# A linear-attention block on one core: the key weights in four transfers instead of three, a shorter dummy matmul, and another order of the first fifteen matmuls and transposes

## The chip, the cores and the metric

The kernel runs on one core of one Trainium2 chip. The time is the device time of one execution in microseconds (us); the profile comes from one profiled execution and gives its span, from the first to the last instruction of the kernel. Engines are named as in the profile: PE is TensorE's matmul, PEld its weight load, DVE is VectorE, ACT is ScalarE, POOL is GpSimd and SP is SyncE. A "q" behind an engine's name (SPq, ACTq) marks the issuing of a transfer by that engine.

## The reference

The block computes linear attention with 32 heads of 20 columns for one sequence of 2048 rows and 640 columns, in bfloat16.

```
qkv = x @ wqkv                      # 2048x640 @ 640x1920, split into q, k, v of 32 heads x 20
phi = lambda t: where(t > 0, t + 1, exp(t)) + 1e-6
pq, pk = phi(q), phi(k)
kv = einsum("bhsd,bhse->bhde", pk, v)
z  = einsum("bhsd->bhd", pk)
o  = einsum("bhqd,bhde->bhqe", pq, kv) / (einsum("bhqd,bhd->bhq", pq, z) + 1e-6)
out = o @ wo
```

## The kernel before, in words

The 2048 rows of x are worked on in 16 row tiles of 128 rows, the 640 inner columns in 5 blocks of 128. A matmul needs x with its columns on the partitions; that form is the tile xT. Row tiles 0 and 1 are loaded as they are (tile xn, L230) and transposed on PE (`transpose_x`, L193 to L213): a low part of two transposes (columns 0 to 255), copied out of PSUM by VectorE (L212), and a high part of three (columns 256 to 639), copied by ScalarE (L209). Rows 256 onwards come as transposing loads on SP's queue (L189).

`k_half` (L284) multiplies a row tile's xT with the key weights Wk: half h (320 of 640 columns) of row tile st, over the inner blocks named in cs. `k_phi` (L298) then applies phi on ScalarE and VectorE. After the keys of all row tiles the kernel accumulates pk and x into a state (L313), computes the queries (L350), forms the product of state, value weights and output weights, divides by the denominator, and multiplies into the output (L572).

Every engine runs its own instructions in the order in which they are written. The class `Plan` notes which instruction wrote and read what, and adds the waits on semaphores. A wait stands ahead of one instruction, and whatever is behind it on that engine waits as well.

What the first microseconds hold:

- `load_wk` (L235) loads x tile 0 ("x01") and x tile 1 ("x12") on SP's queue, and Wk on ScalarE's queue: blocks 0 and 1 in one transfer ("w02"), then blocks 2 and 3 ("w24"), then block 4 ("w45"). Each transfer has its own semaphore. A block of Wk is 128 rows of 640 columns, 160 KB.
- PE first runs dummy matmuls on constants (`warm`, L277): five of 512 columns and one of 256, then the transposes of x tile 0 as they land, then one more dummy of 512 columns (L625).
- Then a written order follows (L626): k and two digits is row tile and inner block, in both halves; a letter a or b behind it picks half 0 or half 1. t1a and t1b are the low and high transposes of x tile 1. Before, it is `k00 k01a t1a k01b t1b k10 k11 k02 k12 k03 k13 k04 k14`. (k01 is row tile 0, inner block 1.)
- K matmuls on inner blocks 0 and 1 of a row tile read the low part of its xT, those on blocks 2 to 4 the high part.

The prediction calls a transpose of the low part "low", one of the high part "high", and the blocks of Wk "block 0" to "block 4".

Of the kernel before, what the change touches and what calls it, by code (L numbers as in the profile page):

```python
# [84 lines left out]
def bass_standalone__linear_attn_block__prompt_kernel(nc, x, wqkv, wo, out):  # L85
# [15 lines left out]
    with contextlib.ExitStack() as ctx:  # L101
# [40 lines left out]
        def bank(b, n=BK, off=0, parts=128):  # L142
            return ps[0:parts, BK * b + off:BK * b + off + n]
# [49 lines left out]
        def transpose_x(st, part):  # L193
            lo, hi = ((0, 2), (2, NC_))[part]
            b = (6, 4)[st] + part
            v = bank(b, HALF).bitcast(BF16)

            def mm(e):
                for c in range(lo, hi):
                    r = e.transpose(  # L200
                        v[:, 128 * c:128 * c + 128],
                        xn[:, st * D + 128 * c:st * D + 128 * c + 128], ident[:, :])
                return r
            P.add("pe", mm, reads=xn_keys(st) + ["ident"], writes=[("bank", b)])
            dst = xT[:, :].rearrange("p (c s) -> p c s", s=S)[
                :, lo:hi, 128 * st:128 * st + 128]
            src = v.rearrange("p (c s) -> p c s", s=128)[:, lo:hi, :]
            if part:
                P.add("act", lambda e: e.copy(dst, src),  # L209
                      reads=[("bank", b), "table"], writes=[("xT", st, lo)])  # L210
            else:
                P.add("dve", lambda e: e.tensor_copy(dst, src),  # L212
                      reads=[("bank", b)], writes=[("xT", st, lo)])  # L213
# [15 lines left out]
        def load_xn(a, b, eng):  # L229
            P.add(eng, lambda e: e.dma_start(  # L230
                xn[:, a * D:b * D].rearrange("p (t n) -> p t n", n=D),
                x[0, 128 * a:128 * b, :].rearrange("(t p) n -> p t n", p=128)),
                writes=[("xn", t) for t in range(a, b)], dma=True)

        def load_wk():  # L235
            tl = mybir.InstLoadActFuncSet(
                name=nc.get_next_instruction_name(),
                act_func_set_id=ACT_TABLE_SET_LN_EXP, ins=[], outs=[])
            P.add("act", lambda e: e.add_instruction(tl), writes=["table"])
            for eng, what in (("sp", "x01 x12"), ("act", "w02 w24 w45")):  # L240
                for k in what.split():
                    a, b = int(k[1]), int(k[2])
                    if k[0] == "x":
                        load_xn(a, b, eng)
                    else:
                        P.add(eng, lambda e, a=a, b=b: e.dma_start(
                            wk[:, a * D:b * D].rearrange("p (c n) -> p c n", n=D),
                            wqkv[128 * a:128 * b, D:2 * D].rearrange("(c p) n -> p c n", p=128)),
                            writes=[("wk", c) for c in range(a, b)], dma=True)
# [27 lines left out]
        def warm(n, cols=BK):  # L277
            for _ in range(n):
                P.add("pe", lambda e: e.matmul(  # L279
                    bank(4, cols), nc.const_aps.tensor(1.0, [128, 128], BF16),  # L280
                    nc.const_aps.tensor(1.0, [128, cols], BF16), start=True, stop=True),
                    writes=[("bank", 4)])
# [333 lines left out]

        pool_const()
        load_wk()
        load_xT()
        load_rest()  # L620
        warm(5)
        warm(1, 256)
        for part in range(2):
            transpose_x(0, part)
        warm(1)  # L625
        order = "k00 k01a t1a k01b t1b k10 k11 k02 k12 k03 k13 k04 k14"  # L626
        for k in order.split():
            st, part = int(k[1]), "ab".find(k[-1])
            if k[0] == "t":
# [127 lines left out]
```

## Time and profile before

| what | value |
|---|---|
| time, median of 3 runs | 99.7 us (99.65 to 99.93) |
| the profiled execution's own time | 99.49 us |
| its span | 98.2 us |
| granted TensorE clock, mean | 1.00 |
| bytes moved | 12.60 MB, 128 GB/s |
| K matmuls (L289) | 160, 22.4 us busy |
| query matmuls (L350) | 95 recorded, 22.0 us busy |
| output matmuls (L572) | 170, 22.1 us busy |
| state matmuls (L313) | 160, 23.2 us busy |

The span leaves out what lies around the kernel's instructions, 1.3 us of the profiled execution's time. A row of the timeline reads: start in us from the span's beginning, duration, engine, line of the kernel, operation, the tile written and the tiles read, shape, and how many instructions are merged in it; where the engine was idle before, the time and what ended it stand in brackets. Matmuls are pipelined: each one's recorded duration is longer than its share of PE's time, so neighbouring rows overlap. In the chain of work that ended last, each piece has its start, its duration and what it is; the chain is followed back from the last instruction, at each step to what released it.

The transfers of the first microseconds, issued and landed by the trace (us):

| transfer | queue | issued | KB | issue to landing |
|---|---|---|---|---|
| x tile 0 | SP | 0.78 | 160 | 2.6 |
| Wk blocks 0, 1 | ACT | 0.80 | 320 | 3.5 |
| x tile 1 | SP | 1.23 | 160 | 3.5 |
| Wk blocks 2, 3 | ACT | 1.29 | 320 | 4.3 |
| Wk block 4 | ACT | 1.82 | 160 | 4.6 |

### The profile page before, as it was taken

What the parts mean: (1) busy time and instruction counts of PE and PEld (TensorE: products, weight loads), DVE (VectorE), ACT (ScalarE), POOL (GpSimd) and SP (SyncE); (2) the same over time, 40 slices, a digit from 0 to 9 for tenths busy, and PEclk for the clock granted to TensorE, in tenths of its full rate; (3) what the DMA queues carried; (4) which work ended last, traced back from release to release, by engine and by line L of the source; (5) the groups of instructions that cost most, each with busy time, mean ns of one, the idle gap of its engine ahead of it and who ended that gap; (6) DMA issues with size and microseconds to landing.
All of it is one profiled execution on the core that took longest, in us unless ns stands there. A gap on an engine that the chain in (4) does not pass through costs nothing.

```text
span 98.2 us, 1813 instructions
## 1 busy us (share of the span) xinstructions
PE 94.8 (97%) x694; PEld 61.1 (62%) x699; DVE 63.7 (65%) x124; ACT 48.8 (50%) x93; POOL 4.7 (5%) x19
## 2 busy tenths in 40 slices
PE   6999999999999999999999999999999999999991
PEld 2467777777755444445687867655557677777771
DVE  5315998898899439997739836759999206272222
ACT  5117455544427120005806456796988665453532
POOL 6400000000000000000000520000000000000000
DMA  2999999999996292000350023313200335532334
GB/s 55 343 263 173 234 211 122 350 366 361 288 166 81 29 256 52 0 0 0 65 75 7 0 63 94 94 33 88 76 0 0 133 81 155 206 124 86 129 133 137
DMA packets 26224, 12.60 MB, mean 128 GB/s; under 512 B 18536, under 2 KB 26216, under 8 KB 26216
## 3 DMA queue, kind: packets, MB, share of 16 engines
q1 hardware_dynamic: 25384, 11.63, 49.9%
q10 hardware_dynamic: 832, 0.86, 2.6%
q8 instruction: 5, 0.08, 0.3%
q14 instruction: 3, 0.02, 0.1%
HBM read 5.90 MB, written 2.62 MB: 87 GB/s over the span
## 4 chain that ended last, share of the span: by engine, by line
PE 92%; DMA 3%; ACT 2%; issue 1%; DVE 0%
PE ps L289 22%; PE ps L572 22%; PE ps L350 22%; PE ps L313 21%; DMA xn<-in_x_dram 3%; ACT w2g L479 2%; PE ps L441 1%; PE ps L540 1%; PE ps L468 1%; PE ps L200 1%; PE ps L279 0%; DVE xT L212 0%; ACT osb L595 0%
## 5 line engine op out<-in xcount | busy, mean ns | idle before, releaser
L313 PE MATMUL ps<-pk,xn 128*128 128x480 bf16 (+1 forms) x160 | 23.2, 299 | 0.0
L289 PE MATMUL ps<-wk,xT 128*128 128x320 bf16 x160 | 22.4, 300 | 0.1
L350 PE MATMUL ps<-xT,wqn 128*128 128x512 bf16 x95 | 22.0, 379 | 0.4 <-issue 0.2
L572 PE MATMUL ps<-w2p,pq 128*128 128x320 bf16 (+2 forms) x170 | 22.1, 291 | 0.0
L572 PEld LDWEIGHTS ps<-w2p,pq 128*128 128x128 bf16 x170 | 15.9, 98 | 6.2 <-issue 0.2
L289 PEld LDWEIGHTS ps<-wk,xT 128*128 128x128 bf16 x160 | 15.7, 98 | 6.5 <-DMA wk<-in_wqkv_dram 0.3
L313 PEld LDWEIGHTS ps<-pk,xn 128*128 128x128 bf16 x160 | 13.6, 98 | 9.4 <-issue 0.3
L358 ACT ACTIVATE eq<-ps 128x512 bf16<-128x512 f32 x20 | 11.9, 597 | 13.8 <-PE ps L350 13.6
L350 PEld LDWEIGHTS ps<-xT,wqn 128*128 128x128 bf16 x100 | 11.4, 118 | 9.1 <-issue 0.3
L302 ACT ACTIVATE ek<-ps 128x640 bf16<-128x640 f32 x16 | 11.2, 704 | 10.5 <-PE ps L289 9.9
L595 ACT CAST osb<-ps 128x320 bf16<-128x320 f32 (+2 forms) x27 | 11.0, 413 | 9.7 <-PE ps L572 8.8
L307 DVE SCALAR_TENSOR_TENSOR pk<-ps,ek 128x640 bf16<-128x640 f32 x16 | 13.2, 825 | 0.5
L565 DVE TENSOR_TENSOR pq<-pq,rd 128x512 bf16<-128x512 bf16 x20 | 7.3, 419 | 4.3 <-DMA rd<-rdc 4.3
L371 DVE TENSOR_SCALAR eq<-eq 128x512 bf16<-128x512 bf16 x20 | 5.7, 287 | 5.9 <-ACT eq L358 5.8
L598 DVE CAST osb<-ps 128x320 bf16<-128x320 f32 (+1 forms) x7 | 3.2, 456 | 8.7 <-PE ps L572 8.7
L304 DVE TENSOR_SCALAR ek<-ek 128x640 bf16<-128x640 bf16 x16 | 5.2, 325 | 4.8 <-ACT ek L302 4.6
L362 ACT ACTIVATE rq<-ps 128x512 bf16<-128x512 f32 x13 | 7.7, 591 | 0.0
L335 ACT CAST pt<-ps 128x480 bf16<-128x480 f32 x4 | 2.3, 563 | 8.2 <-PE ps L313 8.1
L375 DVE TENSOR_TENSOR pq<-eq,rq 128x512 bf16<-128x512 bf16 x13 | 5.5, 425 | 1.1 <-ACT rq L362 0.6
L384 DVE TENSOR_TENSOR za<-pk 128x1280 f32<-128x1280 bf16 x4 | 5.8, 1482 | 0.0
L378 DVE SCALAR_TENSOR_TENSOR pq<-ps,eq 128x512 bf16<-128x512 f32 x7 | 4.8, 692 | 0.2
L384 DVE TENSOR_TENSOR za<-za 128x1280 f32<-128x1280 f32 x3 | 4.4, 1486 | 0.0
(37 smaller groups left out, 36.4 us busy)
## 6 DMA issues: line engine op xcount, KB each, us to landing
out_dram<-osb SPq DMA_DIRECT2D x15, 160.0 KB, 1.8
xn<-in_x_dram SPq DMA_DIRECT2D x2, 640.0 KB, 9.4
xn<-in_x_dram SPq DMA_DIRECT2D x1, 960.0 KB, 7.8
wqn<-in_wqkv_dram SPq DMA_DIRECT2D x1, 800.0 KB, 5.8
wv<-in_wqkv_dram SPq DMA_DIRECT2D x5, 150.0 KB, 5.0
wog<-in_wo_dram SPq DMA_DIRECT2D x2, 375.0 KB, 5.5
w2p<-w2g SPq DMA_DIRECT2D x10, 75.0 KB
wk<-in_wqkv_dram ACTq DMA_DIRECT2D x2, 320.0 KB, 3.9
```

Source lines behind the costliest of these rows:

```text
L289: r = e.matmul(bank(b + h, HALF), xT[:, c * S + 128 * st:c * S + 128 * st + 128], wk[:, c * D + HALF * h:c * D + HALF * (h + 1)], start=(c ...
L302: P.add("act", lambda e: e.activation(fold(t[:, :]), two_banks(b), ACTF.Exp), reads=banks + ["table"], writes=[("ek", st % 3)])
L307: P.add("dve", lambda e: e.scalar_tensor_tensor(fold(pk[:, st * D:(st + 1) * D]), two_banks(b), 0.0, fold(t[:, :]), ALU.max, ALU.add), rea ...
L313: return e.matmul(bank(d // PB[h], PW[h], off=PW[h] * (d % PB[h])), xn[:, st * D + 128 * d:st * D + 128 * d + 128], pk[:, st * D + PO[h]:s ...
L350: r = e.matmul(bank(b), wqn[:, d * D:(d + 1) * D].rearrange("p (q c) -> p c q", c=NC_)[:, c, :], xT[:, d * S + BK * sbk:d * S + BK * (sbk ...
L358: P.add("act", lambda e: e.activation(t[:, :], bank(b), ACTF.Exp), reads=[("bank", b), "table"], writes=[("eq", i)])
L362: P.add("act", lambda e: e.activation(r[:, :], bank(b), ACTF.Relu), reads=[("bank", b), "table"], writes=[("rq", i)])
L371: P.add("dve", lambda e: e.tensor_scalar(t[:, :], t[:, :], 1.0, 1e-6, ALU.min, ALU.add), reads=[("eq", i)], writes=[("eq", i)])
L384: P.add("dve", lambda e: e.tensor_tensor(d_ap, a, b, ALU.add), reads=ra + rb, writes=[dst])
L565: P.add("dve", lambda e: e.tensor_tensor(v, v, rd[i][:, BK * h:BK * (h + 1)], ALU.mult), reads=[("rd", i, 2 * h), ("rd", i, 2 * h + 1), (" ...
L572: r = e.matmul(bank(b, hi - lo), pq[:, c * S + 128 * st:c * S + 128 * st + 128], w2p[:, c * D + lo:c * D + hi], start=(c == 0), stop=(c == ...
L595: P.add("act", lambda e: e.copy(osb[j][:, lo:hi], bank(b, hi - lo)), reads=[("bank", b)], writes=keys)
```

## The change

```diff
@@ load_wk
-            for eng, what in (("sp", "x01 x12"), ("act", "w02 w24 w45")):
+            for eng, what in (("sp", "x01 x12"), ("act", "w01 w12 w24 w45")):
@@ the main sequence
-        warm(1)
-        order = "k00 k01a t1a k01b t1b k10 k11 k02 k12 k03 k13 k04 k14"
+        warm(1, 128)
+        order = "k00 t1a k01 k10a t1b k10b k11 k02 k12 k03 k13 k04 k14"
```

Wk's blocks 0 and 1 come in a transfer each, so ScalarE issues four transfers instead of three, and the first matmul on block 1 gets a wait of its own. The dummy matmul ahead of the K matmuls has 128 columns instead of 512. The low transposes of x tile 1 move one matmul earlier, right behind the two matmuls of row tile 0 on block 0; both halves of block 1 follow; then half 0 of row tile 1 on block 0 (k10a, which needs VectorE's copy of the low part), then the high transposes, then half 1 (k10b). On PE this moves 6 rows of the first 20 (the number of K matmuls and transposes stays); on ScalarE one transfer is added; VectorE, GpSimd and SyncE have the same instructions in the same order.

## The prediction, as it was put on record

> **What bounds the kernel now.** I read the engine table first, then the chain of work that ended last, then the first 7 us instruction by instruction, because every edit lies there. Engine table and shares of the chain, from the page:
>
> ```profile
> PE 94.8 (97%) x694; PEld 61.1 (62%) x699; DVE 63.7 (65%) x124; ACT 48.8 (50%) x93; POOL 4.7 (5%) x19
> ...
> PE 92%; DMA 3%; ACT 2%; issue 1%; DVE 0%
> ```
>
> PE is busy for 97% of the span and carries 92% of the chain. So what the change does to PE's start is carried to the end nearly one for one, if nothing later absorbs it. The chain in order of time, first 14 us:
>
> ```profile
> 0.78 2.64 DMA xn<-in_x_dram
> 3.42 0.05 issue
> 3.47 0.71 PE ps L200 x5
> 4.18 0.43 PE ps L279
> 4.61 0.54 PE ps L289 x3
> 5.15 0.12 PE ps L200 x2
> 5.28 0.02 issue
> 5.30 0.30 DVE xT L212
> 5.60 0.05 issue
> 5.65 8.46 PE ps L289 x61
> ```
>
> The reader sees: x tile 0 lands at 3.42, PE transposes it, then the dummy matmul (L279) and three K matmuls follow, then the low transposes of x tile 1 and their copy on VectorE, for which PE waits. From 5.65 on PE runs through. The PE rows of the timeline there:
>
> ```profile
> 3.98 0.63 PE L279 MATMUL ps<-const-bfloat16-1.0 128*128 128x512 bf16 x1
> ...
> 4.40 0.75 PE L289 MATMUL ps<-wk,xT 128*128 128x320 bf16 x3
> 4.99 0.28 PE L200 MATMUL ps<-ident,xn 128*128 128x128 bf16 x2
> 5.10 0.30 PE L289 MATMUL ps<-wk,xT 128*128 128x320 bf16 x1
> 5.24 0.33 PE L200 MATMUL ps<-ident,xn 128*128 128x128 bf16 x3
> 5.65 0.31 PE L289 MATMUL ps<-wk,xT 128*128 128x320 bf16 x1
> ```
>
> The single starts within these groups, from the same view in narrower windows, are 4.40, 4.67, 4.85 (K), 4.99, 5.04 (low transposes), 5.10 (K), 5.24, 5.29, 5.35 (high transposes), then 5.65, 5.80, 5.93, 6.07, 6.20, 6.34, 6.47 (K). Durations overlap, so I count from start to start. A K matmul takes 0.27 at first and 0.135 later (5.80 to 6.20 holds three); a transpose takes 0.055 later; the first matmul after a wait takes 0.15. The matmul after the one of 4.67 began 0.18 later: 0.09 at the slow rate and 0.09 at the fast one, so the rate doubled at about **4.76**, 3.94 after the first matmul (0.82). The granted clock reads 1.00 in every stretch and doesn't show this; the spacing does.
>
> **Dummy matmul, 512 to 128 columns.** It begins at 3.98 and releases PE at 4.40 (0.42 at the slow rate). A quarter of it takes 0.11, so PE is free at 4.09: 0.31 removed. What is late next is VectorE's copy of the low part of x tile 0 (3.90 + 0.29 = 4.19). After the like copy at 5.30 (ending 5.59) the released matmul began at 5.65, 0.06 later; here two waits stand before it, and the copy's and the block's waits took 0.04 each, so 0.10: first K matmul at 4.29. Gain at this point 0.11, not 0.31. Bounds: 0.15 if the waits cost 0.06; 0 if the block were still late.
>
> **Wk in four transfers.** Landings by the trace's completion records: x tile 0 at 3.42, Wk blocks 0 and 1 at 4.28, x tile 1 at 4.76, blocks 2 and 3 at 5.64, block 4 at 6.37. The records of the packets show how they are served: on each DMA engine the first packet of x tile 1 follows the last of blocks 0 and 1 (3.54 after 3.54 on the first engine to finish, though x tile 1 was issued at 1.23). So transfers pass one after the other, alternating between SP's and ACT's queue, and half of blocks 0 and 1 is 8 packets of 55 ns on an engine: 0.44. Splitting them puts x tile 1 ahead of block 1. Estimates: block 0 lands at 4.28 - 0.44 = 3.84, x tile 1 at 4.76 - 0.44 = 4.32, block 1 at 4.76, the rest where they were. A transfer more on ACT's queue takes 0.49 (the issue durations are 0.46, 0.49 and 0.49 us): blocks 2 and 3 are issued at 1.78 instead of 1.29, block 4 at 2.27 instead of 1.82. Behind these issues on ACT stands the copy of x tile 0's high part, which begins at 4.22 and waits for PE; issues ending at 2.76 leave 1.4 of cover. Blocks 2 and 3 would be served from 3.96, block 4 from 4.79, 1.7 and 2.0 after their issues end; the shortest such delay in the trace is 0.63 (x tile 0). So I take zero. Upper bound: 0.49 late each, to land at 6.13 and 6.86; they are needed at 6.19 and 7.29, so still zero. SP's queue issues the same as before.
>
> Smaller transfers could also cost a fixed time each; here transfers issued 0.5 apart (x tile 1 after x tile 0, blocks 2 and 3 after 0 and 1, block 4 after those) land 1.34, 1.36 and 0.73 apart, their packets without a gap between, so I see no such cost and take none. [...]
>
> **The order on PE.** K block 0 in both halves: 4.29, 4.56. At 4.76 0.20/0.27 of the second is done, and the rest takes 0.04: PE is free at 4.80. Low transposes at 4.80 and 4.86 (x tile 1 is there from 4.32). Block 1's two matmuls at 4.91 and 5.05, PE free at 5.18. The copy started 0.26 after the second transpose (5.04 to 5.30) and the released matmul 0.35 after that: copy at 5.12, K at **5.47**, against 5.65. But before, the high transposes lay ahead of that wait; now PE idles 0.29 (0.25 before) and they come behind it: 5.47 + 0.15 = 5.62, 5.67, 5.73. Then K at 5.78, 5.92, 6.05 and block 2 at 6.19 and 6.32; block 2 of tile 1 could begin at 6.46, but reads the high part, which ScalarE copies 0.25 after the third transpose (5.35 to 5.60) in 0.48 and releases 0.06 later: 5.73 + 0.79 = **6.52**. Before, the same matmul began at 6.47. So the copy hidden before by 0.8 us of K work now ends last, by 0.06, and what was won before 5.65 is given back. Sum: -0.18 (5.65 to 5.47), +0.165 (three transposes moved behind the wait), +0.06: about **+0.05 us**. Behind it, block 3 (5.64) and block 4 (6.37) are there, x tile 2's transposing load lands at 6.9 and is needed at 7.9. Nothing later is moved, and +0.05 goes to the end.
>
> Profiled time 99.49 (span 98.2) + 0.05 = 99.54. The runs' median is 99.7, 0.21 above the profiled execution, so in terms of the median 99.75. A change below 0.3% (0.3 us, about what a measurement of this kernel can tell) is "no change".
>
> **Rivals.**
> 1. *Slower: the rate doubles later.* PE had one idle stretch of 0.15 (3.32 to 3.47) in the 3.94 us before 4.76. The change adds 0.20 (4.09 to 4.29). If the doubling follows the amount of busy work, it comes 0.2 later: about +0.1, partly hidden in the idle 0.29. If it needs an unbroken 3.94 us from 4.29, it comes at 8.23: 3.47 us at half rate cost 1.73, less the waits that vanish (0.29 and 0.06), +1.4: 101.1. It decides (over 0.3%) from a delay of some 0.8. For it: the dummies are the only work that covers the landing. Against: the 0.15 already there did no visible harm. Chance 0.16. [...]
> 2. *Faster: timed runs have later landings than the profile.* Before, x tile 1 landed 0.23 ahead of its use; from landings 0.2 later on, the kernel before pays one for one, while the changed one has 0.44 more. To come out 0.3 faster, the landings must be 0.55 later than in the profile, for 99.4. The median lies only 0.21 above. Chance 0.10, with anything else that helps.
> 3. *The split doesn't move x tile 1 ahead.* Then its transposes wait for 4.76, begin at 4.82, and the whole is +0.07: no change.
> 4. *Blocks 2 and 3 are served after x tile 2's transposing load* (some 0.95 us of packets from 5.13): they would land 0.4 after their use. Against: SP's queue moved nothing from 4.34 to 5.13, so that load was not ready. Chance 0.02.
>
> **How the numbers follow.** No change 0.72 (the forecast, rival 3, small delays of the doubling), slower 0.18 (rivals 1 and 4), faster 0.10. Range 99.4 (rival 2) to 100.3 (a doubling some 1.5 us late); beyond it lies the full form of rival 1.
>
> **What would show it.** After: first K matmul near 4.29; low transposes near 4.80; K behind VectorE's copy near 5.47 with an idle of 0.29; PE waiting up to 0.1 for ScalarE's copy near 6.5; starts 0.135 apart from 4.8 on. Spacing of 0.27 beyond 5.2 is rival 1; a wait on Wk near 6.2 is rival 4. If the first K matmul comes well before 4.2, or the high copy isn't last, my sum is wrong.

## The result

The changed kernel takes 101.13 us (median of 6 runs, 100.51 to 101.82) beside 99.68 us for the kernel before (6 runs, 99.56 to 100.12): a ratio of 1.0128, 95% interval 1.0096 to 1.0160. It is slower by 1.3%, where no change was forecast, with 99.75 us and a range up to 100.3. On another chip (the first of the last four experiments) the whole change gave 1.0122 (1.0079 to 1.0165).

The ratios leave out executions more than 1.5% above the fastest of the same kernel as disturbed; in some kernels below such executions belong to the effect, so medians, means and counts over all executions stand beside the ratios. For the count: none of the 116 executions of the kernel before in this study took more than 100.70 us.

### The profile page after: what moved, and what is told of

It is laid out like the page before. It is cut to its first block, busy times and chain, and to the rows that moved or that the text cites. A ratio compares the mean times of both kernels' runs of the same rounds, so it can differ in the third digit from the quotient of the medians.

```text
span 99.3 us, 1819 instructions
## 1 busy us (share of the span) xinstructions
PE 95.9 (97%) x699; PEld 61.3 (62%) x699; DVE 63.7 (64%) x124; ACT 48.7 (49%) x93; POOL 4.7 (5%) x19
## 3 DMA queue, kind: packets, MB, share of 16 engines
HBM read 5.90 MB, written 2.62 MB: 86 GB/s over the span
## 4 chain that ended last, share of the span: by engine, by line
PE 94%; DMA 3%; ACT 0%; issue 0%
PE ps L289 23%; PE ps L572 22%; PE ps L313 22%; PE ps L350 22%; DMA xn<-in_x_dram 3%; PE ps L441 1%; PE ps L540 1%; PE ps L200 1%; PE ps L468 1%; ACT osb L595 0%; PE ps L279 0%
## 5 line engine op out<-in xcount | busy, mean ns | idle before, releaser
L289 PE MATMUL ps<-wk,xT 128*128 128x320 bf16 x160 | 23.2, 306 | 0.0
L350 PE MATMUL ps<-xT,wqn 128*128 128x512 bf16 x100 | 23.1, 379 | 0.0
```

The lines of the kernel that those rows point to most:

```text
L289: r = e.matmul(bank(b + h, HALF), xT[:, c * S + 128 * st:c * S + 128 * st + 128], wk[:, c * D + HALF * h:c * D + HALF * (h + 1)], start=(c ...
L350: r = e.matmul(bank(b), wqn[:, d * D:(d + 1) * D].rearrange("p (q c) -> p c q", c=NC_)[:, c, :], xT[:, d * S + BK * sbk:d * S + BK * (sbk ...
```

## The profile after

The engine table and the shares of the chain, from the page of the changed kernel (its profiled execution took 100.51 us, its span is 99.3):

```profile
PE 95.9 (97%) x699; PEld 61.3 (62%) x699; DVE 63.7 (64%) x124; ACT 48.7 (49%) x93; POOL 4.7 (5%) x19
...
PE 94%; DMA 3%; ACT 0%; issue 0%
```

PE is as full as before (97%), and holds still more of the chain. A busy PE alone doesn't tell that it got slower. The chain in order of time (start, duration, what):

```profile
0.79 3.01 DMA xn<-in_x_dram
3.79 0.05 issue
3.84 0.71 PE ps L200 x5
4.55 0.11 PE ps L279
4.66 0.05 issue
4.71 0.69 PE ps L289 x2
5.40 0.21 PE ps L200 x2
5.62 0.83 PE ps L289 x3
6.45 0.32 PE ps L200 x3
6.77 7.28 PE ps L289 x52
```

Two things differ from before. The first piece, the landing of x tile 0, ends at 3.79 instead of 3.42. And VectorE's copy, a piece of the chain before, is gone from it: two transposes now take 0.21 and three 0.32, at the slow rate, and PE itself is the limit. PE's rows of the timeline:

```profile
2.91 0.42 PE L279 MATMUL ps<-const-bfloat16-1.0 128*128 128x256 bf16 x1
3.84 0.71 PE L200 MATMUL ps<-ident,xn 128*128 128x128 bf16 x5 [0.51 <-DMA xn<-in_x_dram]
4.35 0.31 PE L279 MATMUL ps<-const-bfloat16-1.0 128*128 128x128 bf16 x1
4.71 0.69 PE L289 MATMUL ps<-wk,xT 128*128 128x320 bf16 x2
5.20 0.42 PE L200 MATMUL ps<-ident,xn 128*128 128x128 bf16 x2
5.41 1.04 PE L289 MATMUL ps<-wk,xT 128*128 128x320 bf16 x3
6.24 0.53 PE L200 MATMUL ps<-ident,xn 128*128 128x128 bf16 x3
6.56 3.69 PE L289 MATMUL ps<-wk,xT 128*128 128x320 bf16 x24
```

The bracket in the second row is the idle ahead of the transposes, 0.51; before there was none long enough to be listed. The last row hides a step: the starts of its first matmuls are 6.56, 6.83 and 7.09 (0.27 apart) and then 7.23, 7.37, 7.50 (0.135 apart). So the rate doubled at 7.09 instead of 4.76. The granted clock is 1.00 here as well.

**Where the 1.02 us of this execution went.** I take the start of the twentieth K matmul, the last one of row tiles 0 and 1, as a milestone. It is 7.70 before and 8.73 after. From there to the start of the last output matmul both take 88.34 (96.04 - 7.70 and 97.07 - 8.73), and in every profile of this study 88.3 to 88.4, so the whole difference lies ahead of it. It splits by the starts of PE's instructions: the first transpose is later by 0.37 (3.47 and 3.84); the work at the slow rate costs 0.84 more (1.49 instead of 0.65 above the fast rate); the shorter dummy saves an estimated 0.16 at the fast rate (384 columns fewer, where 320 take 0.135); waits between instructions change by 0.03 (0.25 and 0.22). 0.37 + 0.84 - 0.16 - 0.03 = 1.02.

The transfers by the trace's completion records: x tile 0 at 3.79 (before 3.42), block 0 at 3.99, x tile 1 at 4.50 (4.76), block 1 at 4.80, blocks 2 and 3 at 5.73 (5.64), block 4 at **7.68** (6.37). Block 4 was in time here only because PE was late itself: its first use came at 8.32, where before it came at 7.29.

## Theories

**S**: the split makes x tile 0 land later, PE idles longer ahead of the transposes, and this delays the doubling. **D**: the shorter dummy alone delays it. **B** (after the first four runs): the split makes the later Wk blocks fall in with the transposing loads, and PE waits for them.

## Experiments: one edit at a time

**Only the split.**

```diff
-... ("act", "w02 w24 w45")
+... ("act", "w01 w12 w24 w45")
```

> Only the four Wk transfers; dummy of 512 columns and order as before. Theory S (the split makes x tile 0 land later, 3.79 instead of 3.42, PE idles 0.51 instead of 0.15 ahead of its transposes, and that idle delays the doubling of PE's rate): x tile 0 lands near 3.8, the rate doubles near 7.1 instead of 4.76, time 100.5 to 101.8 like the whole change. Theory D (the shorter dummy alone takes PE below the activity that doubles the rate): the rate doubles near 4.8, and the time is 99.7 to 100.0, whatever x tile 0 does.

Measured: 101.25 us (100.73 to 101.77) beside 100.06; ratio 1.0127 (1.0092 to 1.0162). x tile 0 landed at 3.96, the rate doubled at 7.92. The split alone loses as much as the whole change. But its trace shows something that S doesn't have: blocks 2 and 3 landed at 7.11, block 4 at 9.0, and PE waited for block 4 (a spacing of 0.33 at 8.71).

**Only the shorter dummy.**

```diff
-        warm(1)
+        warm(1, 128)
```

> Only the dummy of 128 instead of 512 columns; transfers and order as before. Theory D: doubling 2 us or more later than 4.76, time 100.5 to 101.8. Theory S: x tile 0 lands near 3.42, doubling near 4.8, time 99.6 to 99.8 (PE waits for Wk blocks 0 and 1 until 4.33, so at most 0.07 is gained). If both are needed, this one and the split alone are each near 99.7 and only the whole change is slow.

Measured: ratio 0.9995 (0.9969 to 1.0020), median 100.16 beside 100.06, x tile 0 at 3.43, doubling at 5.40. D falls as the cause of the whole. But the executions are in two groups: eight from 99.61 to 100.39, and four from 101.17 to 101.78. The short dummy now and then costs over 1 us: the mean of all twelve is 100.44 beside 100.01. None of the four was profiled, so that the rate doubled late in them is not shown.

**Only the order.**

```diff
-        order = "k00 k01a t1a k01b t1b k10 k11 k02 ..."
+        order = "k00 t1a k01 k10a t1b k10b k11 k02 ..."
```

> Only the new order of K matmuls and transposes; dummy of 512 columns and three Wk transfers. Both theories: doubling near 4.8, since what PE does up to there is nearly the same. By the sums of the prediction the high copy then ends last and the time is 99.7 to 99.9 (+0.05 to +0.15). If the order alone gives 100.5, both theories fall.

Measured: ratio 1.0005 (0.9983 to 1.0026), 99.79 to 100.52. In its trace the rate doubled at 5.09, PE stood 0.28 behind VectorE's copy (forecast 0.29) and 0.055 behind ScalarE's copy of the high part (forecast 0.06). The order does what the prediction worked out, and costs nothing that can be measured.

**The split and the order, with the dummy of 512.**

```diff
-        warm(1, 128)
+        warm(1)
```

(The edits of this and the following kernels are against the whole change, where nothing else is said.)

> The whole change but with the dummy of 512 columns. Theory D: the doubling is back near 4.8 and the time is 99.6 to 99.9. Theory S: x tile 0 lands near 3.8, doubling near 7, time 100.5 to 101.8.

Measured: median 100.55 beside 100.06, ratio 1.0034 (1.0004 to 1.0065); 99.83 to 101.65, three of twelve above 101. Neither theory fits: some executions are as good as before, others as bad as the whole change. The profiled one (101.65) shows both losses at once, doubling at 7.09, then a short wait of PE for blocks 2 and 3 (0.14; they landed at 7.35) and a long one for block 4, which landed at 9.39:

```profile
6.61 2.04 PE L289 MATMUL ps<-wk,xT 128*128 128x320 bf16 x11
9.44 0.85 PE L289 MATMUL ps<-wk,xT 128*128 128x320 bf16 x5 [0.78 <-DMA wk<-in_wqkv_dram]
```

Counted from start to start, block 4 cost PE 0.94. So theory B was added. The mean of all twelve is 100.56 beside 100.01: less than half of what the split alone lost (101.32), and of what the whole change loses (101.25 beside 99.99 in its second measurement). So the short dummy has a part in the whole change's loss, and the split costs less with the new order than with the old one; no run follows up why.

## Experiments: idle, filling, and the later Wk blocks

**The kernel before with more idle ahead of the transposes.**

```diff
 # against the kernel before
-        warm(5)
+        warm(4)
         warm(1, 256)
```

> The kernel before with four instead of five of the first dummies (512 columns): no transfer changes, and PE idles some 0.43 us longer (0.78 instead of 0.35, counted from the end of the last dummy's share) ahead of x tile 0's transposes, as the split made it. Theory S (idle ahead of the transposes delays the doubling): time 100.7 to 101.8, doubling near 7 to 8. Theory B (the split costs by Wk block 4 landing late, behind the transposing load): x tile 0 still lands near 3.45, block 4 near 6.4, time as before, within 0.2.

Measured: ratio 1.0019 (0.9988 to 1.0051), median 100.28 beside 99.92; ten of twelve from 99.54 to 100.78, two at 101.49 and 102.31. The idle between the dummies and the transposes is 0.67 here, counted from the end of the last dummy's share of PE's time; by the same count it is 0.35 before and 0.72 in the changed kernel. S as I had it falls: such an idle by itself costs over 1 us only now and then, and in the profiled execution the doubling came at 4.32. (The two long executions were not profiled.)

**The whole change with seven dummies, which leave no idle.**

```diff
-        warm(5)
-        warm(1, 256)
+        warm(7)
```

> The whole change with seven dummies of 512 columns instead of five and one of 256, which end near 3.76, so PE has next to no idle ahead of the transposes although x tile 0 lands late. Theory S: the doubling is back at 4.8 to 5.2, and what is left over before is the wait for block 4, if any: 99.9 to 100.6. Theory B: no gain over the whole change: 101 to 101.4.

Measured: 101.06 (100.73 to 101.41) beside 99.92; ratio 1.0119 (1.0084 to 1.0154), no better than the whole change. Yet the doubling came at 6.0. PE's timeline shows what took its place:

```profile
6.30 0.57 PE L289 MATMUL ps<-wk,xT 128*128 128x320 bf16 x3
7.44 1.26 PE L289 MATMUL ps<-wk,xT 128*128 128x320 bf16 x8 [0.56 <-DMA wk<-in_wqkv_dram]
8.90 1.40 PE L289 MATMUL ps<-wk,xT 128*128 128x320 bf16 x9 [0.20 <-DMA wk<-in_wqkv_dram]
```

Counted from start to start, PE lost 0.73 for blocks 2 and 3 (landed at 7.39) and 0.36 for block 4 (8.85). A faster PE arrives earlier at blocks that are late.

**The same, with blocks 2 to 4 in one transfer.**

```diff
-... "w01 w12 w24 w45"
+... "w01 w12 w25"
```

> As the kernel with seven dummies, and Wk blocks 2 to 4 in one transfer (four blocks' transfers become three: 1, 1 and 3 blocks), issued third on ScalarE's queue. Both theories count here if their shares add: doubling near 5, blocks 2 to 4 landing near 6.4 to 7, time 99.6 to 100.0. Theory S alone: like the kernel with seven dummies, within 0.2. Theory B alone: 0.5 or more below it but still late doubling.

Measured: 101.25 (100.95 to 103.47), ratio 1.0142 (1.0098 to 1.0187). In its profiled execution the rate had doubled by 3.76, the earliest of all, and the time is as bad as ever:

```profile
5.77 0.57 PE L289 MATMUL ps<-wk,xT 128*128 128x320 bf16 x3
7.87 2.35 PE L289 MATMUL ps<-wk,xT 128*128 128x320 bf16 x16 [1.53 <-DMA wk<-in_wqkv_dram]
```

The one large transfer landed at 7.82: on some DMA engines its last packet had passed at 5.17, on others at 7.45; the transposing loads' packets had begun at 5.18. This is B without any clock in it. My expectation that the larger transfer would be through by 7 was wrong.

**The first Wk transfer issued later.**

```diff
-... "w01 w12 w24 w45"
+... "w01 w12 w25"
-   ... writes=[("wk", c) for c in range(a, b)], dma=True)
+   ... writes=[("wk", c) for c in range(a, b)], dma=True,
+       after=[P.writers["ident"]] if a == 0 else [])
```

> The whole change, but ScalarE issues its first Wk transfer some 0.7 us later (behind GpSimd's making of the identity), so that block 0 doesn't share the DMA engines with x tile 0, and Wk comes as 1, 1 and 3 blocks. Dummies as in the whole change (idle ahead of the transposes 0.35 again, dummy of 128 columns). If sharing is what delays x tile 0, it lands near 3.45 again. Theory S: doubling at 4.8 to 5.5 in most executions, time 99.7 to 100.2, with a spread like that of the short dummy alone (99.6 to 101.8). If x tile 0 lands near 3.8 all the same, the delay isn't from sharing.

Measured: 104.51 (102.31 to 105.34), the worst of all. It answers one question: with no Wk packets beside it (they began at 2.76, when its last had passed at 2.55), x tile 0 landed at 3.01. So block 0's transfer, issued beside it, is what delays it. But now x tile 1 was through by 3.2, the transposing loads' packets began at 3.42, and every Wk transfer crawled: block 0 landed at 4.98, block 1 at 7.42, and PE stood 1.7 for block 1 alone.

## Experiments: block 4 moved, dummies, a later block 4

**Block 4 ahead of the transposing loads on SP's queue.**

```diff
-... (("sp", "x01 x12"), ("act", "w01 w12 w24 w45"))
+... (("sp", "x01 x12 w45"), ("act", "w01 w12 w24"))
```

> The whole change, but Wk block 4 is issued on SP's queue ahead of the transposing loads (third there) instead of fourth on ScalarE's. Theory B (Wk bytes not yet moved when the transposing loads start, at 4.4 to 5.2, crawl): blocks 2 to 4 land by 6.6, no wait for Wk on PE after 6, and the executions of 101.3 to 101.8 vanish: median 100.0 to 100.6. Theory S/D (only the doubling of PE's rate counts): median stays at 101.0 to 101.3.

Measured: ratio 1.0036 (1.0004 to 1.0068), median 100.68 beside 100.06. Seven executions lie from 99.72 to 100.71, five from 101.72 to 102.01. In the trace block 4 landed at 6.46. Blocks 2 and 3, still on ScalarE's queue, landed at 7.21 (expected by 6.6), which cost PE at most 0.12 there: the matmul that needs them began at 7.25, 0.25 after the one ahead of it, and the rate doubled somewhere between the two. The expected vanishing of the executions above 101.3 didn't come about: they are five of twelve. The ratio is near 1 only because it leaves those five out: the mean of all twelve is 100.97 beside 100.03. So this kernel shows B's cure only in part.

**The same with seven dummies.**

```diff
-        warm(5)
-        warm(1, 256)
+        warm(7)
```

> The same with seven dummies of 512 columns, so that PE has next to no idle ahead of the transposes either. If the change's loss is the sum of late Wk blocks and a late doubling, this one is back at the kernel before: 99.6 to 100.1, doubling at 3.8 to 6.1. If seven dummies do nothing for the doubling, it equals the kernel with block 4 on SP's queue.

Measured: ratio 1.0007 (0.9982 to 1.0033), 99.55 to 100.53, no execution above. Doubling by 4.66, blocks 2 and 3 at 6.15, block 4 at 5.65. With both cures the loss is gone, though the split, the short dummy and the new order are all still there.

**The kernel before with six dummies.**

```diff
 # against the kernel before
-        warm(5)
-        warm(1, 256)
+        warm(6)
```

> The kernel before with six dummies of 512 columns instead of five and one of 256: the first transposes find PE busy to 3.33, x tile 0 lands at 3.42. Theory S: the doubling can only come earlier or as before: 99.5 to 99.9, and less spread than before (99.5 to 100.7). If idle ahead of the transposes doesn't matter: within 0.1 of before.

Measured: ratio 0.9984 (0.9955 to 1.0013), 99.45 to 100.36. No difference that can be told. In its profiled execution the doubling came as late as 6.37, with PE waiting nowhere between the first transpose and the twentieth K matmul. x tile 0 landed at 3.67 there, so PE had idled 0.38 ahead of the transposes all the same.

**The kernel before with block 4 issued later.**

```diff
 # against the kernel before
-   ... writes=[("wk", c) for c in range(a, b)], dma=True)
+   ... writes=[("wk", c) for c in range(a, b)], dma=True,
+       after=[P.writers["hm"]] if a == 4 else [])
```

> The kernel before, but ScalarE issues Wk block 4 some 0.7 us later (at 2.55 instead of 1.82, behind a step of GpSimd's), with everything else as before, x tile 0's landing included. Theory B: block 4 falls in with the transposing loads and lands at 7.5 to 9, needed at 7.3: PE waits 0.2 to 1.5 for it, time 100.2 to 101.3. Theory S/D: it still lands by 7.3, and the time is as before within 0.2.

Measured: ratio 0.9999 (0.9975 to 1.0023), 99.66 to 100.44. In the profiled execution block 4 landed at 7.90 and PE lost 0.46 to it, as B expects, but the timed executions don't show it. So a late issue of block 4 alone isn't enough.

## Experiments: holding the transposing loads back

**The whole change again**, for comparison on the same chip:

> The whole change once more, on the chip of the next three kernels: 100.6 to 101.3. In its trace either Wk blocks late (after 6.2 for blocks 2 and 3, after 8 for block 4) or a late doubling (7 to 8), or both.

Measured: 101.23 (100.87 to 101.68) beside 99.97, ratio 1.0122 (1.0079 to 1.0165). Its profiled execution (101.68) had the rate double only at 9.47. Fifteen K matmuls take 3.62 in the last row, where in the same stretch the first profile had 24 in 3.69:

```profile
6.26 0.53 PE L200 MATMUL ps<-ident,xn 128*128 128x128 bf16 x3
6.58 3.62 PE L289 MATMUL ps<-wk,xT 128*128 128x320 bf16 x15
```

**Held loads.** The first transposing load waits until x tile 0 has landed; all Wk transfers stay where the change put them.

```diff
     writes=[("xT", NPE + i)], dma=True)
+    # as an argument of the same call
+    after=[P.writers[("xn", 0)]] if i == 0 else []
```

> The whole change, with SP's first transposing load waiting for x tile 0 to land (issued near 3.8 instead of 1.7). Theory B (their traffic makes Wk late): blocks 2 and 3 land by 5.8, block 4 by 6.8, no wait for Wk, and the time falls to that of the kernel with block 4 on SP's queue, 100.0 to 100.6. If the place as fourth transfer is what matters: block 4 lands at 7.5 to 9.4 still, time as the whole change.

Measured: ratio 1.0045 (1.0006 to 1.0085), median 100.49; 99.78 to 101.97, five of twelve above 101. The transposing loads' packets began at 5.38 (4.97 in the whole change), blocks 2 and 3 landed at 5.77 and block 4 at 6.48, though it is still the fourth transfer on ScalarE's queue. So it is the loads' traffic, not the place in the queue. PE's last row up to 10 us holds 24 K matmuls without a wait (starts at 6.54, 6.80, 7.02, 7.16, and 0.136 apart from there):

```profile
6.54 3.64 PE L290 MATMUL ps<-wk,xT 128*128 128x320 bf16 x24
```

The doubling came at 6.97; that is what is left in this execution (100.42), with no wait for Wk. The five above 101 were not profiled.

**Held loads and seven dummies.**

```diff
-        warm(5)
-        warm(1, 256)
+        warm(7)
```

> The same with seven dummies of 512 columns. If the loss is late Wk plus late doubling: 99.7 to 100.3, no execution above 101. If the dummies do nothing: like the one before it.

Measured: ratio 1.0000 (0.9974 to 1.0025), 99.62 to 100.31. The loss is gone a second time, by another cure for B. In the chain VectorE's copy is back, the piece by which PE was limited before the change:

```profile
5.40 0.13 PE ps L201 x2
5.52 0.02 issue
5.54 0.30 DVE xT L213
5.85 0.05 issue
5.89 0.31 PE ps L290
```

(Its lines are numbered one higher.)

**The kernel before with held loads.**

> The kernel before, with the transposing loads held back alike. Wk was not late there, so holding can gain nothing through Wk; it costs if x tiles 2 and 3 come late (they are needed at 7.8 and 9.2 and would land near 7.2 and 8.6): within 0.2 of before.

Measured: ratio 0.9993 (0.9963 to 1.0024), 99.34 to 100.57. Holding back costs and gains nothing by itself.

## What the runs settle

The loss of 1.2% has two causes, and each hides the other:

| kernel | ratio (95%) | mean of all (before) | above 101 us |
|---|---|---|---|
| the whole change (second chip) | 1.0122 (1.0079 to 1.0165) | 101.25 (99.99) | 4 of 6 |
| seven dummies only | 1.0119 (1.0084 to 1.0154) | 101.07 (99.96) | 4 of 6 |
| block 4 on SP's queue only | 1.0036 (1.0004 to 1.0068) | 100.97 (100.03) | 5 of 12 |
| held loads only | 1.0045 (1.0006 to 1.0085) | 100.69 (99.99) | 5 of 12 |
| block 4 on SP's queue, seven dummies | 1.0007 (0.9982 to 1.0033) | 100.16 (100.03) | 0 of 12 |
| held loads, seven dummies | 1.0000 (0.9974 to 1.0025) | 100.00 (99.99) | 0 of 12 |

*Late Wk blocks.* What of Wk has not moved when the transposing loads' packets begin moves slowly. In the kernel before those packets began at 5.13, when blocks 2 and 3 and a third of block 4 (0.34) had passed; block 4 landed at 6.37. In the whole change they began at 4.97 in both profiles, just as the first DMA engine was through with blocks 2 and 3, and block 4 landed at 7.68 and 8.04. Where PE ran fast early, it waited for Wk (0.73 + 0.36 with seven dummies); where PE ran slow for long, it didn't wait, because it was late itself.

*A late doubling of PE's rate.* Without the split the doubling came at 4.32 to 6.74 in seven profiles; with the split and no filling at 6.97 to 9.47 in six (one of them known only to lie from 7.0 to 7.25); with the split and seven dummies at 3.76 to 6.0 in four. (Where the first Wk transfer was issued later, PE stood for over a microsecond twice, and the rate doubled only at 12.88.) Filling the idle cures it: with it and B cured, no execution of 24 lies above 101. A longer idle alone (2 of 12 above 101) and a short dummy alone (4 of 12) each cost over 1 us now and then, by a late doubling as I read it, though no such execution was profiled; with the split they come together.

*Why x tile 0 is late.* With the split it landed at 3.50 to 3.96 in ten profiles (mean 3.76), without it at 3.30 to 3.67 in seven (mean 3.47), alone at 3.01 (one profile). The issue of the smaller Wk transfer takes 0.39 instead of 0.46, and its packets may begin as early as 1.99 (2.32 at the earliest without the split), when x tile 0 has most of its own to come. That isn't all of it: in both profiles of the whole change they began at 2.6, and x tile 0 was as late. In the first of them 18 packets began between 1.8 and 2.4 us, all of x tile 0, where before it was 91; what held them up is not shown.

**Open:** what PE must have done for its rate to double. The times scatter by 2.4 us without the split, with nothing on PE that goes with it: 6.37 came with 0.38 of idle ahead of the transposes and no wait behind them, 4.32 with 0.67 of idle. With seven dummies the rate had doubled by 3.76 in one profile, 2.94 after the first matmul. Open as well is how far the two causes share the loss in a typical execution, since filling the idle alone moves nothing, and holding the loads alone moves 0.8 of the 1.2% by the ratios, 0.7 of the 1.3 us by the medians and 0.6 of the 1.3 us by the means. No version here beats the kernel before beyond its interval.

## Why the prediction was wrong, point by point

- **What bounds the kernel, and that a shift at the start goes to the end**: right, to 0.1 us in every profile (88.3 to 88.4 from the milestone on).
- **"So transfers pass one after the other"**: failed. For x tile 1 the step held in kind (it landed at 4.50, forecast 4.32, before 4.76). But the step was read off a block of two, whose packets came when x tile 0 was mostly through: 85 of its 128 packets had passed when the first of them began, at 2.43. In the changed kernel's profile 22 of the 128 had passed when block 0's first packet began, at 2.62, and from 2.6 to 3.2 as many packets of the one began as of the other (87 each). The prediction kept x tile 0 at 3.42, and it was 3.79: the first term missing from the sum, +0.37 in this execution.
- **"Blocks 2 and 3 ... block 4 ... So I take zero"**: failed. The bound of 0.49 late each (6.13 and 6.86) counted the later issue alone. Block 4 landed at 7.68 and 8.04. Rival 4 had the mechanism, and got a chance of 0.02 on the ground that SP's queue moved nothing from 4.34 to 5.13. That showed when the loads began in one execution, not by how much the change had to lose to be caught; and it left out that the loads behind an earlier x tile 1 can begin earlier (4.44 to 5.18 with the split and unheld loads, and 3.42 where x tile 1 was earliest; 4.79 to 5.55 without the split; that x tile 1 sets this is read from these times, not tested).
- **The doubling at 4.76 as a fixed point**: failed, and it is the largest term in both profiles of the change (+0.84 in the first). It came from one execution, and from a favourable one: its 99.49 us lie below all 116 executions of the kernel before (99.51 to 100.70), and six further profiles without the split doubled from 4.32 to 6.74. Rival 1 named the mechanism and its price (a doubling at 8.23, +1.4), but counted only the 0.20 of idle behind the dummy. With x tile 0 late, the idle ahead of the transposes was 0.51 by the timeline instead of 0.15. By the timeline's rows the same idle is smaller than by the count used above, since a row lasts longer than its share (0.63 against 0.42 for the dummy at 3.98 before). The median of 101.13 is what that rival gave in its full form (101.1), for half of its reason and by luck: the two profiles of the change doubled at 7.09 and 9.47, not at 8.23.
- **The dummy's 0.11 and the order's +0.05**: right in kind. The dummy alone and the order alone change no median (the dummy alone adds 0.4 to the mean, by its four long executions); VectorE's idle of 0.29 and ScalarE's 0.06 were measured at 0.28 and 0.055. In the changed kernel's profile the wait behind the first copy was 0.15 instead of 0.10, and behind the second PE idled only 0.06, because it came late at the slow rate.
- **"I see no such cost and take none"**, of a fixed cost for each transfer: no run shows such a cost, and fewer, larger transfers were no better: with one of 480 KB in place of two for blocks 2 to 4 the time was 101.25, with the two 101.06. What the runs show in its place is that transfers of SP's and ScalarE's queues hold each other up: x tile 0 landed at 3.01 with no Wk packets beside it, and at 3.79 and 3.82 in the whole change; block 4 landed at 6.48 with the transposing loads held back, and at 7.68 and 8.04 without.

## What to carry to other kernels

When a transfer is split or moved, write down for every transfer beside it who is served before and after, the ones you don't touch first of all: here x tile 0, ahead of the split, and block 4, behind it, paid for an earlier x tile 1 that PE didn't need. A point in time that comes from one profiled execution, such as the moment at which PE's rate doubles, is a draw and not a constant; look at how the runs scatter before building on it. And if curing one cause moves nothing, cure the suspected second one too before dropping the first.

## What was not expected of the hardware

- One of the transposing loads' neighbours can be slowed out of proportion: a Wk transfer of 480 KB was through at 5.17 on the first DMA engine and at 7.45 on the last, once the transposing loads' 256-byte packets had begun at 5.18.
- The doubling of PE's rate differed by 5.7 us between executions and kernels (3.76 to 9.47, and 12.88 where PE stood for Wk twice), with a granted clock of 1.00 in all of them; only the spacing of the matmuls shows it.
- A small transfer issued at the same moment can cost the one that is waited for: x tile 0 landed at 3.01 alone (one profile), at 3.47 on average beside a transfer of 320 KB, and at 3.76 beside one of 160 KB.
